# Retention and a gelu feed-forward in one kernel: the first four units in 128-token steps, with another load order

## The chip, the core and the metric

The kernel runs on one core of a Trainium2 chip. The metric is device time in microseconds (us). Four runs of the kernel before gave 297.36, 299.20, 298.86 and 299.65 us, median 299.03. The profile is that of the first of them.

A core has five engines that run beside each other: TensorE (PE in the profile, with its weight loads as PEld), VectorE (DVE), ScalarE (ACT), GpSimd (POOL) and SyncE (SP). They wait for each other through semaphores. TensorE writes its results to PSUM, eight banks of 128 partitions by 512 fp32 numbers, which DVE and ACT read. Here POOL issues the loads and SP the stores.

## What is computed

```
scale = 1/sqrt(64);  gamma[h] = 1 - 2^(-5-h)
scores = scale * q @ k^T                      # q, k, v: 8 batches, 8 heads, 576 tokens, 64 wide, fp32
ret    = (scores * gamma[h]^(i-j) for i >= j, else 0) @ v
x      = ret, heads side by side              # 4608 tokens x 512
h      = x @ w_in                             # 512 x 2048
out    = (h * sigmoid(1.702 h)) @ w_out       # 2048 x 512, fp32 out
```

The decay factorizes: a row is multiplied by gamma^i and v by gamma^-j. So attention can go in blocks, and all earlier blocks enter through one 64x64 state per head, the sum of k^T v.

## The kernel before, in words

The 4608 tokens are 36 units of 128. Four units make a chunk, and there are nine chunks. Units 0 to 3 are the first 512 tokens of batch 0, so each of them needs the state of the ones before. For a chunk, the up-projection makes 16 column blocks of 128 (`up`, L532, one block for all 512 tokens with four matmuls; `up_group`, L545, several blocks for some of the units), each followed by a gelu on ACT (L541, L555). Then `down` (L560) makes four output tiles of 128 tokens, and `down_out` copies and stores them. The attention of the units of the next chunk is placed between these matmuls by hand.

There is no planner. Every operation is written out in order by `op` (L41); each engine runs its own operations in that order, and the waits follow from the names that an operation reads and writes. TensorE waits for TensorE only where `after_ops` says so.

The change is in `lead_in` (L662), which loads and attends units 0 to 3 and makes chunk 0.

- Loads. SP loads k and q of unit 0 (`load_kq0`, L232). POOL issues, in one queue: v of unit 0; k, q, v of unit 1 (`load`, with `load_kq` L208 and `load_v` L222); `load_win(0)` (L251), which is 512 columns of w_in in two transfers, one for each 64 partitions; unit 2; `load_win(1)`; unit 3; `load_win(2)` and `(3)`; four transfers of w_out; then units 4 to 11. k and q are turned from fp32 into bf16 on the way, and so is w_in.
- Transposes. `transpose_pe` (L341) makes four 128x128 transposes of k, or of q, into a bank, and `transpose_copy` (L349) brings them to `kqT` on ACT or DVE.
- Scores. `scores` (L471): a unit is two halves of 64 tokens. Each half is scored with itself only: 16 matmuls of 64x64 over four tiles of the array, head halves to banks C and D. `scores_out` (L484) multiplies them by the causal mask on DVE into `pm`.
- States. `state_half` (L390) adds one half's k^T v to bank K (eight matmuls, L383), and ACT casts the bank into `kv` (L393). This is done after each half.
- `block1` (L589): `inter` (L446) multiplies each half's q by the state before that half (16 matmuls of 64x64; for the second half that is the state after the first); `values` (L492) adds scores times v in two phases, where the second phase waits for the last matmul of the first, so that two row halves of the array don't write the same part of a bank at once; between the phases stands the second half's state. `x_out` (L511) multiplies banks X and Y by gamma^i on DVE into `xT`, the input of the up-projection.
- `warm` (L652) is a filler: a matmul of zeros into a bank that nobody reads. L654 in the profile.

In `lead_in` the order on TensorE is: seven fillers, unit 0, unit 1, five fillers, up of blocks 0 to 3 for units 0 and 1, unit 2, blocks 4 to 7 for units 0 and 1, unit 3 with blocks 0 to 7 for unit 2 between its steps, blocks 8 to 11 for all four units, blocks 0 to 7 for unit 3, and blocks 12 to 15 whole. Then the down-projection of chunk 0 begins, with units 4 to 7 attended between its steps.

Of the kernel before, what the change touches and what calls it, by code (L numbers as in the profile page):

```python
# [6 lines left out]
AF = mybir.ActivationFunctionType  # L7
# [6 lines left out]
P = 128  # L14
# [110 lines left out]
def unit_info(u):  # L125
    pb, i = divmod(u, 9)
    if i < 4:
        return pb, 0, i
    if i < 8:
        return pb, 1, i - 4  # L130
    return pb, 2, 4
# [12 lines left out]
def head(pb, g, hh):  # L144
    return 4 * pb + 2 * g + hh
# [13 lines left out]
def bass_retnet_parallel__then__act_gelu_quick_kernel(  # L159
# [10 lines left out]
    with es:  # L170
        def sb(name, shape, dtype):
            return es.enter_context(nc.sbuf_tensor(name, shape, dtype))
# [9 lines left out]
        kqT = [sb(f"kqT{i}", [P, 2 * HP, P], BF16) for i in range(NQT)]  # L182
        vp = [sb(f"vp{i}", [P, H, DH], BF16) for i in range(NVP)]
        pm = [[sb(f"pm{i}_{hh}", [P, 512], BF16) for hh in range(2)] for i in range(2)]
        kv = sb("kv", [P, NKV, HP, DH], BF16)
        stm = sb("stm", [P, 8, HP, DH], FP32)
        xT = [sb(f"xT{i}", [P, 4, 512], BF16) for i in range(2)]
# [11 lines left out]
        def ps32(n):  # L199
            return bank[n].ap()  # L200
# [47 lines left out]
        def kq_pair(u, which, hp):  # L248
            return kqn[u % NLD][:, which, 2 * hp : 2 * hp + 2, :]

        def load_win(i):  # L251
            op("pool", lambda e: [e.dma_start(
                w_in_sb[64 * pb : 64 * pb + 64, :, 512 * i : 512 * i + 512],
                moe_w_in[256 * pb : 256 * pb + 256, 512 * i : 512 * i + 512].rearrange(
                    "(a d) n -> d a n", d=DH),
            ) for pb in range(2)], writes=[f"win{i}"], dma=f"d_win{i}", ndma=2)

        def load_wout(i):
            op("pool", lambda e: e.dma_start(
# [116 lines left out]
        def key(u, a):  # L376
            return (2 * u + a) % NKV

        def update(u, a, banks, col, first):
            sl = u % NLD  # L380
            for hp in range(HP):
                for hh in range(2):
                    op("pe", lambda e, hp=hp, hh=hh: e.matmul(  # L383
                        ps32(banks[a])[64 * hh : 64 * hh + 64, col + 64 * hp : col + 64 * hp + 64],
                        kqn[sl][64 * a : 64 * a + 64, 0, 2 * hp + hh, :],
                        vp[u % NVP][64 * a : 64 * a + 64, 2 * hp + hh, :],
                        start=first and hp == 0, stop=True, skip_group_check=True),
                       reads=[f"kq{sl}_0", f"vp{u % NVP}"], writes=[banks[a]])

        def state_half(u, a):  # L390
            pb, kind, c = unit_info(u)
            update(u, a, "KK", 0, c == 0 and a == 0)
            op("act", lambda e: e.activation(  # L393
                kv[:, key(u, a), :, :].rearrange("p a i -> p (a i)"), ps32("K")[:, 0:256], AF.Copy),
               reads=["K"], writes=[f"kv{key(u, a)}"])

        KB = "KE"

# [72 lines left out]
        def scores(u):  # L471
            qt = kqT[u % NQT]
            c0 = 256 * (u % 2)
            for hp in range(HP):
                for a in range(2):
                    for hh in range(2):
                        op("pe", lambda e, hp=hp, a=a, hh=hh: e.matmul(  # L477
                            ps32(SB[hh])[64 * a : 64 * a + 64, c0 + 64 * hp : c0 + 64 * hp + 64],
                            qt[64 * hh : 64 * hh + 64, hp, 64 * a : 64 * a + 64],
                            qt[64 * hh : 64 * hh + 64, HP + hp, 64 * a : 64 * a + 64],  # L480
                            skip_group_check=True),
                           reads=[f"T{u % NQT}_0", f"T{u % NQT}_1"], writes=[SB[hh]])
# [49 lines left out]
        def up(c, f, lo=0, hi=4, b=None):  # L532
            b = b or "AB"[f % 2]
            n0, n1 = P * lo, P * hi
            for a in range(4):
                op("pe", lambda e, a=a: e.matmul(  # L536
                    bank[b][:, n0:n1], w_in_sb[:, a, P * f : P * f + P], xT[c % 2][:, a, n0:n1],
                    start=(a == 0), stop=(a == 3)),
                   reads=[f"win{f // 4}"] + [f"x{c % 2}_{j}_{hh}" for j in range(lo, hi) for hh in range(2)],
                   writes=[b])  # L540
            op("act", lambda e: e.activation(  # L541
                gT[c % 2][:, f, n0:n1], bank[b][:, n0:n1], AF.Gelu_apprx_sigmoid),
               reads=[b], writes=[f"g{c % 2}_{f}_{j}" for j in range(lo, hi)])

        def up_group(c, f0, nf, lo, hi, b):  # L545
            n = P * (hi - lo)
            for i in range(nf):
                f = f0 + i
                for a in range(4):
                    op("pe", lambda e, a=a, f=f, i=i: e.matmul(  # L550
                        bank[b][:, n * i : n * i + n], w_in_sb[:, a, P * f : P * f + P],
                        xT[c % 2][:, a, P * lo : P * hi], start=(a == 0), stop=(a == 3), skip_group_check=True),
                       reads=[f"win{f // 4}"] + [f"x{c % 2}_{j}_{hh}" for j in range(lo, hi) for hh in range(2)],
                       writes=[b])
            op("act", lambda e: e.activation(  # L555
                gT[c % 2][:, f0 : f0 + nf, P * lo : P * hi],
                bank[b][:, 0 : n * nf].rearrange("p (f t) -> p f t", f=nf), AF.Gelu_apprx_sigmoid),
               reads=[b], writes=[f"g{c % 2}_{f}_{j}" for f in range(f0, f0 + nf) for j in range(lo, hi)])
# [22 lines left out]
            return op("sp", f, reads=[f"osb{i}_{n0}"], writes=[f"out{u}_{n0}"],  # L581
                      dma=f"d_o{i}_{n0}", ndma=len(unit_rows(u)))

        def score1(u):
            scores(u)
            scores_out(u, 1, 0)
            scores_out(u, 1, 1)

        def block1(u, xo=True):  # L589
            started.clear()  # L590
            inter(u, u % 2)
            o = values(u, u % 2, 0)
            if unit_info(u)[1] < 2:
                state_half(u, 1)
            values(u, u % 2, 1, [o])
            if xo:
                x_out(u, u % 2, 0)
                x_out(u, u % 2, 1)

        def ahead(j):  # L600
            if 2 * j < NU:
# [60 lines left out]
        def lead_in():  # L662
# [3 lines left out]
            iota_large()  # L666
            load_v(0)
            load(1)
            load_win(0)
            load(2)  # L670
            load_win(1)
            load(3)
            load_win(2)
            load_win(3)
            for i in range(4):
                load_wout(i)
            for u in range(4, NPE + 4):
# [11 lines left out]
            cast_kq0(1, "dve")  # L689
            transpose_pe(0, 0, "E")  # L690
            transpose_copy(0, 0, "E", "dve")
            warm(1)
            transpose_pe(0, 1, "B")
            transpose_copy(0, 1, "B", "dve")
            scale_v(0)
            warm(2)
            scores(0)
            scores_out(0, 1, 0)
            scores_out(0, 1, 1)
            gq_next(1)  # L700
            state_half(0, 0)
            transpose_pe(1, 0, "E")
            transpose_copy(1, 0, "E", "act")
            warm(2)
            transpose_pe(1, 1, "B")
            transpose_copy(1, 1, "B", "act")
            scale_v(1)
            block1(0)
            warm(1)
            scores(1)  # L710
            scores_out(1, 1, 0)
            scores_out(1, 1, 1)
            warm(4)
            state_half(1, 0)
            warm(2)
            block1(1)
            warm(5)
            up_group(0, 0, 2, 0, 2, "A")
            up_group(0, 2, 2, 0, 2, "B")
            transpose_pe(2, 0, "E")  # L720
            transpose_copy(2, 0, "E", "dve")
            warm(1, "C")
            transpose_pe(2, 1, "D")
            transpose_copy(2, 1, "D", "act")
            warm(3, "C")
            scores(2)
            scale_v(2)
            scores_out(2, 1, 0)
            scores_out(2, 1, 1)
            gq_next(2)  # L730
            warm(2)
            state_half(2, 0)
            warm(2)
            block1(2)
            gq_next(3)
            up_group(0, 4, 2, 0, 2, "A")
            up_group(0, 6, 2, 0, 2, "B")
            transpose_pe(3, 0, "E")
            transpose_copy(3, 0, "E", "dve")
            transpose_pe(3, 1, "D")  # L740
            transpose_copy(3, 1, "D", "act")
            scale_v(3)
            up_group(0, 0, 4, 2, 3, "A")
            scores(3)
            state_half(3, 0)
            scores_out(3, 1, 0)
            scores_out(3, 1, 1)
            up_group(0, 4, 4, 2, 3, "B")
            block1(3)
            up_group(0, 8, 2, 0, 2, "A")  # L750
            up_group(0, 10, 2, 0, 2, "B")
            up_group(0, 8, 2, 2, 4, "A")
            up_group(0, 10, 2, 2, 4, "B")
            up_group(0, 0, 4, 3, 4, "A")
            up_group(0, 4, 4, 3, 4, "B")
            gq_next(4)
            gq_next(5)
            for f in range(12, NF):
                up(0, f)
            def ahead45():  # L760
                ahead(2)
# [151 lines left out]
```

## Time and profile before

| what | value |
|---|---|
| median of the four runs | 299.03 us |
| the profiled execution | 297.36 us |
| its span, first to last instruction | 295.6 us |
| TensorE busy | 289.3 us, 98% |
| ACT, DVE, POOL busy | 133.1, 100.8, 108.1 us |
| first up-projection matmul of chunk 0 (L550) | 13.20 us |
| first down-projection matmul (L562) | 32.84 us |
| granted TensorE clock | 1.00 |

A page of the profile gives, for each engine, busy time and instruction count; then the span in 40 slices of 7.4 us with the busy share in tenths; then the chain that ended last, which goes from the last instruction back to whatever released it; then groups of instructions by line of code. A timeline row has a start and a length in us, the engine, the line, the operation, the tile written and the tiles read, the shapes, and in brackets how long the engine had been idle and who ended that. Matmuls are pipelined: a row's length includes the way through the array, so the pace is read from the starts.

### The profile page before, as it was taken

To read this page: it belongs to the slowest core of one execution; us is meant where nothing else is said; L and a number is where in the kernel's file an instruction comes from. 1 tells how busy PE (TensorE), PEld (TensorE's weight loads), DVE (VectorE), ACT (ScalarE), POOL (GpSimd) and SP (SyncE) were. 2 spreads that over 40 slices of the span, in tenths; PEclk is the share of its full clock that TensorE was granted. 3 is DMA by queue.
4 is the path that set the end of the run, shared out by engine and by line. 5 is a ranking of instruction groups with operands and counts; after the bars stand their busy time and mean duration, and the time that the engine had idled before them with its cause. 6 is when DMAs were issued, how large, how long until landed. Compare 5 with 4: busy or idle time off the path is not lost.

```text
span 295.6 us, 7921 instructions
## 1 busy us (share of the span) xinstructions
PE 289.3 (98%) x3584; PEld 141.7 (48%) x3584; DVE 100.8 (34%) x203; ACT 133.1 (45%) x233; POOL 108.1 (37%) x137
## 2 busy tenths in 40 slices
PE   7999999899999999999999999999999999999996
PEld 2578355775543454345434543454345434443344
DVE  7464046444571344034602470138004700410000
ACT  7456434563347324732464246423652375216511
POOL 9999498000960940390029301920090000000000
PEclk9999999999999999999999999999999999999999
DMA  9999999996999993699369926991993050110021
GB/s 163 180 208 206 206 234 249 235 148 144 159 226 188 137 219 112 120 178 166 99 127 140 192 90 144 158 200 50 171 100 97 27 137 0 38 73 35 0 73 71
DMA packets 117234, 40.63 MB, mean 137 GB/s; under 512 B 106064, under 2 KB 110416, under 8 KB 117200
## 3 DMA queue, kind: packets, MB, share of 16 engines
q0 software_dynamic: 80160, 22.81, 67.0%
q1 hardware_dynamic: 37040, 17.31, 22.0%
q8 instruction: 28, 0.46, 0.6%
q14 instruction: 6, 0.05, 0.1%
HBM read 36.70 MB, written 9.44 MB: 156 GB/s over the span
## 4 chain that ended last, share of the span: by engine, by line
PE 96%; DMA 2%; POOL 1%; issue 1%; DVE 0%; POOLq 0%
PE psA L562 22%; PE psB L562 21%; PE psA L536 17%; PE psB L536 17%; PE psB L550 4%; PE psA L550 4%; PE psX L461 2%; DMA kqn<-in_q_dram 2%; PE psA L654 1%; PE psC L477 1%; PE psY L499 1%; PE psX L499 1%; PE psK L406 1%; PE psD L477 1%; PE psE L406 1%
## 5 line engine op out<-in xcount | busy, mean ns | idle before, releaser
L214 POOL DMA_DIRECT2D kqn<-in_k_dram x39 | 35.3, 915 | 111.4 <-DMA kqT<-kqn 108.3
L562 PE MATMUL psA<-w_out_sb,gT 128*128 128x512 bf16 (+1 forms) x304 | 70.1, 374 | 0.0
L562 PE MATMUL psB<-w_out_sb,gT 128*128 128x512 bf16 (+1 forms) x288 | 64.6, 373 | 0.0
L536 PE MATMUL psA<-xT,w_in_sb 128*128 128x512 bf16 x232 | 59.5, 379 | 0.0
L536 PE MATMUL psB<-xT,w_in_sb 128*128 128x512 bf16 x232 | 59.5, 379 | 0.0
L524 DVE TENSOR_TENSOR xT<-psX,gq 128x512 bf16<-128x512 f32 x16 | 11.1, 692 | 120.5 <-PE psX L499 120.5
L430 ACT ACTIVATE kv<-stm 128x1024 bf16<-128x1024 f32 (+1 forms) x18 | 15.6, 866 | 68.4 <-DVE stm L421 68.4
L562 PEld LDWEIGHTS psB<-w_out_sb,gT 128*128 128x128 bf16 x288 | 27.8, 98 | 31.7 <-ACT gT L541 0.3
L562 PEld LDWEIGHTS psA<-w_out_sb,gT 128*128 128x128 bf16 x304 | 27.8, 98 | 31.5 <-ACT gT L541 2.5
L541 ACT ACTIVATE gT<-psB 128x512 bf16<-128x512 f32 x58 | 34.6, 597 | 15.3 <-PE psB L536 15.2
L541 ACT ACTIVATE gT<-psA 128x512 bf16<-128x512 f32 x58 | 34.6, 597 | 14.9 <-PE psA L536 14.9
L227 POOL DMA_DIRECT2D vn<-in_v_dram x40 | 37.4, 942 | 1.4 <-issue 1.3
L214 POOL DMA_DIRECT2D kqn<-in_q_dram x39 | 35.5, 921 | 0.0
L536 PEld LDWEIGHTS psA<-xT,w_in_sb 128*128 128x128 bf16 x232 | 18.6, 97 | 31.3 <-ACT gT L541 16.0
L536 PEld LDWEIGHTS psB<-xT,w_in_sb 128*128 128x128 bf16 x232 | 18.1, 97 | 32.0 <-ACT gT L541 15.7
L336 DVE TENSOR_TENSOR vp<-vn,vfac 128x512 bf16<-128x512 f32 x36 | 23.2, 685 | 16.4 <-DMA vn<-in_v_dram 16.4
L572 ACT ACTIVATE osb<-psB 128x512 f32<-128x512 f32 (+1 forms) x18 | 10.5, 585 | 21.5 <-PE psB L562 21.5
L572 ACT ACTIVATE osb<-psA 128x512 f32<-128x512 f32 x18 | 10.5, 584 | 15.3 <-PE psA L562 15.3
L486 DVE TENSOR_TENSOR pm<-psC,mask 128x512 bf16<-128x512 f32 (+1 forms) x20 | 12.6, 629 | 8.8 <-PE psD L477 8.7
L550 PE MATMUL psB<-xT,w_in_sb 128*128 128x256 bf16 (+1 forms) x128 | 14.8, 260 | 0.1
L550 PE MATMUL psA<-xT,w_in_sb 128*128 128x256 bf16 (+1 forms) x128 | 14.6, 259 | 0.0
L486 DVE TENSOR_TENSOR pm<-psD,mask 128x512 bf16<-128x512 f32 (+1 forms) x20 | 12.6, 628 | 0.0
(76 smaller groups left out, 257.2 us busy)
## 6 DMA issues: line engine op xcount, KB each, us to landing
vn<-in_v_dram POOLq DMA_DIRECT2D x32, 256.0 KB, 5.4
out_dram<-osb SPq DMA_DIRECT2D x31, 256.0 KB, 2.1
kqn<-in_k_dram POOLq DMA_DIRECT2D x31, 128.0 KB, 4.9
kqn<-in_q_dram POOLq DMA_DIRECT2D x31, 128.0 KB, 5.0
w_in_sb<-in_moe_w_in_dram POOLq DMA_DIRECT2D x8, 256.0 KB, 8.6
w_out_sb<-in_moe_w_out_dram POOLq DMA_DIRECT2D x4, 512.0 KB, 15.7
out_dram<-osb SPq DMA_DIRECT2D x10, 128.0 KB, 2.5
vn<-in_v_dram POOLq DMA_DIRECT2D x8, 128.0 KB, 5.1
```

Source lines behind the costliest of these rows:

```text
L214: e.dma_start(kqn[sl][p0 : p0 + n, which, :, :], src[b, :, s0 : s0 + n, :].rearrange("h p d -> p h d"),)
L227: e.dma_start(vn[sl][p0 : p0 + n, :, :], v[b, :, s0 : s0 + n, :].rearrange("h p d -> p h d"))
L336: op(eng, lambda e: e.tensor_tensor(vp[u % NVP].ap(), vn[sl].ap(), vfac[:, ty, :, None].to_broadcast([P, H, DH]), ALU.mult), reads=[f"vn{s ...
L406: op("pe", lambda e, hp=hp, a=a, hh=hh: e.matmul(ps32(KB[a])[64 * hh : 64 * hh + 64, c0 + 64 * hp : c0 + 64 * hp + 64], kqn[sl][64 * a : 6 ...
L430: op("act", lambda e: e.activation(kv[:, i0 % NKV : i0 % NKV + n, :, :], stm[:, i0 % 8 : i0 % 8 + n, :, :], AF.Copy), reads=[f"stm{(i0 + i ...
L486: op("dve", lambda e: e.tensor_tensor(pm[(u0 // 2) % 2][hh][:, c0:c1].rearrange("p (a i) -> p a i", i=64), ps32(SB[hh])[:, c0:c1].rearrang ...
L524: op("dve", lambda e: e.tensor_tensor(xT[ch % 2][:, slice(hh, 4, 2), P * jj : P * jj + 2 * P].rearrange("p g (u t) -> p u g t", u=2), ps32 ...
L536: op("pe", lambda e, a=a: e.matmul(bank[b][:, n0:n1], w_in_sb[:, a, P * f : P * f + P], xT[c % 2][:, a, n0:n1], start=(a == 0), stop=(a == ...
L541: op("act", lambda e: e.activation(gT[c % 2][:, f, n0:n1], bank[b][:, n0:n1], AF.Gelu_apprx_sigmoid), reads=[b], writes=[f"g{c % 2}_{f}_{j ...
L550: op("pe", lambda e, a=a, f=f, i=i: e.matmul(bank[b][:, n * i : n * i + n], w_in_sb[:, a, P * f : P * f + P], xT[c % 2][:, a, P * lo : P * ...
L562: op("pe", lambda e, f=f: e.matmul(bank[b][:, 0 : n1 - n0], gT[c % 2][:, f, P * r : P * r + P], w_out_sb[:, f, n0:n1], start=(f == 0), sto ...
L572: op("act", lambda e: e.activation(dst, src, AF.Copy), reads=[b], writes=[f"osb{i}_{n0}"])
```

## The change

Units 0 to 3 are attended as whole 128-token steps. The state goes from unit to unit only: `state1` adds a whole unit's k^T v at once (eight matmuls with all 128 tokens as rows) and `state1_cast` casts it once. `inter1` multiplies the q of all 128 tokens by the state after the unit before. What the second half takes from the first half of its own unit now comes from cross scores: `scores1` makes eight matmuls of 64x64 more into bank B, four before the usual sixteen and four behind them, where the second four wait for the last of the first four; `cross_out` copies them to a new tile `pmx` on ACT; `cross_values` multiplies them with v at the end of each phase of `values1`. The second phase waits for the last cross value of the first.

POOL's queue loads unit 2 right behind unit 1, then the columns of w_in for blocks 0 and 1, then unit 3, then blocks 2 and 3, 4 and 5, 6 and 7 in pairs, and 8 to 11 and 12 to 15 in fours as before. The wait of an up-projection is now for its own block's columns. The order on TensorE is written anew, with fillers at other places.

```diff
-        def load_win(i):
+        def load_win(f0, nf):
             op("pool", lambda e: [e.dma_start(
-                w_in_sb[64 * pb : 64 * pb + 64, :, 512 * i : 512 * i + 512],
+                w_in_sb[64 * pb : 64 * pb + 64, :, P * f0 : P * f0 + P * nf],
...
+        def state1(u):
...
+                        ps32("K")[64 * hh : 64 * hh + 64, 64 * hp : 64 * hp + 64],
+                        kqn[sl][:, 0, 2 * hp + hh, :], vp[u % NVP][:, 2 * hp + hh, :],
...
+        def scores1(u):
+            qt = kqT[u % NQT]
+            o = None
+            for hh in range(2):
+                if hh:
+                    scores(u)
+                wait = [o] if hh else ()
+                for hp in range(HP):
+                    o = op("pe", lambda e, hp=hp, hh=hh: e.matmul(
+                        ps32("B")[0:64, 256 * hh + 64 * hp : 256 * hh + 64 * hp + 64],
+                        qt[64 * hh : 64 * hh + 64, hp, 0:64],
+                        qt[64 * hh : 64 * hh + 64, HP + hp, 64:128], skip_group_check=True),
+                       reads=[f"T{u % NQT}_0", f"T{u % NQT}_1"], writes=["B"], after_ops=wait)
...
+        def cross_out(u):
+            dst = pmx[0:64, u % 2, :]
+            op("act", lambda e: e.activation(dst, ps32("B")[0:64, :], AF.Copy),
+               reads=["B"], writes=[f"pmx{u % 2}"])
...
+        def values1(u, phase, after_ops=()):
...
+            return cross_values(u, phase)
...
+        def block1(u):
             started.clear()
-            inter(u, u % 2)
-            o = values(u, u % 2, 0)
-            if unit_info(u)[1] < 2:
-                state_half(u, 1)
-            values(u, u % 2, 1, [o])
+            if u % 4:
+                inter1(u)
+            o = values1(u, 0)
+            values1(u, 1, [o])
+            x_out(u, u % 2, 0)
+            x_out(u, u % 2, 1)
...
             load(1)
-            load_win(0)
             load(2)
-            load_win(1)
+            load_win(0, 2)
             load(3)
-            load_win(2)
-            load_win(3)
+            load_win(2, 2)
+            load_win(4, 2)
+            load_win(6, 2)
+            load_win(8, 4)
+            load_win(12, 4)
```

The new order of `lead_in` from unit 0's scores to the down-projection (calls on TensorE, DVE and ACT in the order in which they are issued):

```
scores1(0); scores1_out(0, 0); scores1_out(0, 1); cross_out(0); warm(1, "A")
transpose_pe(1, 0, "E"); transpose_copy(1, 0, "E", "act"); state1(0); block1(0)
transpose_pe(1, 1, "A"); transpose_copy(1, 1, "A", "act"); state1_cast(0); scale_v(1); warm(2, "C")
scores1(1); scores1_out(1, 0); scores1_out(1, 1); cross_out(1); warm(1, "A")
transpose_pe(2, 0, "E"); transpose_copy(2, 0, "E", "act"); state1(1); gq_next(1); warm(1, "A"); block1(1)
transpose_pe(2, 1, "A"); transpose_copy(2, 1, "A", "act"); state1_cast(1); scale_v(2); warm(3, "C")
scores1(2); scores1_out(2, 0); scores1_out(2, 1); cross_out(2); gq_next(2); warm(3, "E"); block1(2)
gq_next(3); warm(2, "C"); up_group(0, 0, 2, 0, 2, "A")
transpose_pe(3, 0, "E"); transpose_copy(3, 0, "E", "dve"); transpose_pe(3, 1, "D"); transpose_copy(3, 1, "D", "dve")
scale_v(3); up_group(0, 0, 2, 2, 3, "B"); state1(2); state1_cast(2); warm(1, "C")
scores1(3); scores1_out(3, 0); scores1_out(3, 1); cross_out(3); warm(4, "E"); block1(3)
up_group(0, 2, 2, 0, 2, "A"); up_group(0, 2, 2, 2, 3, "B"); state1(3); state1_cast(3)
up_group(0, 0, 4, 3, 4, "E"); gq_next(4); gq_next(5); up(0, 4) to up(0, 15)
```

Here `up_group(c, f0, nf, lo, hi, bank)` makes blocks f0 to f0+nf-1 for units lo to hi-1. From the down-projection of chunk 0 on, nothing is changed.

## Prediction

> **What bounds the kernel now.** I read the page first: engine shares and slices, then the chain that ended last.
>
> ```profile
> PE 289.3 (98%) x3584; PEld 141.7 (48%) x3584; DVE 100.8 (34%) x203; ACT 133.1 (45%) x233; POOL 108.1 (37%) x137
> ...
> PE   7999999899999999999999999999999999999996
> ...
> DMA  9999999996999993699369926991993050110021
> ...
> PE 96%; DMA 2%; POOL 1%; issue 1%; DVE 0%; POOLq 0%
> ```
>
> TensorE is the bound and carries 96% of the chain; DMA carries 2%, all of it before 8.1 us (unit 1's q). So only what lengthens or shortens TensorE's own order counts. The change stops at the first down-projection: from there both orders are the same. The question is therefore when the first L562 row starts. In TensorE's timeline:
>
> ```profile
> 11.99 1.25 PE L654 MATMUL psA<-gT 128*128 128x512 bf16 x5
> 13.20 1.05 PE L550 MATMUL psA<-xT,w_in_sb 128*128 128x256 bf16 x8
> 14.08 1.04 PE L550 MATMUL psB<-xT,w_in_sb 128*128 128x256 bf16 x8
> 14.95 0.39 PE L344 MATMUL psE<-ident,kqn 128*128 128x128 bf16 x4
> ...
> 32.84 1.03 PE L562 MATMUL psA<-w_out_sb,gT 128*128 128x512 bf16 x4
> ```
>
> It starts at 32.84. Chunk 0's up-projection is 16 column blocks at 0.86 (starts 30.25, 31.11, 31.97): 13.8 us in either kernel. The other 19 us are attention for units 0 to 3, filler matmuls (L654), and waits; only these can change. The fillers here stand where unit 2's data is awaited. DVE's timeline shows that release:
>
> ```profile
> 16.12 0.69 DVE L336 TENSOR_TENSOR vp<-vn,vfac 128x512 bf16<-128x512 f32 x1 [0.32 <-DMA vn<-in_v_dram]
> ```
>
> The short rows I price with come from the end of unit 1's block:
>
> ```profile
> 11.35 0.21 PE L461 MATMUL psX<-kqT,kv 64*64 64x64 bf16 x1
> ...
> 11.53 0.19 PE L499 MATMUL psY<-pm,vp 64*64 64x64 bf16 x1
> 11.56 0.29 PE L383 MATMUL psK<-vp,kqn 64*64 64x64 bf16 x8
> 11.81 0.22 PE L499 MATMUL psY<-pm,vp 64*64 64x64 bf16 x2
> ...
> 11.87 0.20 PE L499 MATMUL psX<-pm,vp 64*64 64x64 bf16 x2
> 11.99 0.39 PE L654 MATMUL psA<-gT 128*128 128x512 bf16 x1
> ```
>
> Read starts, not lengths (matmuls overlap). Sixteen L461 take 0.14, eight L499 0.07, eight L383 0.11. A matmul that waits for an earlier TensorE matmul starts 0.28 after that one's start (11.53 to 11.81). Going back to full-array work costs 0.12 to 0.13 after the last start (11.87 to 11.99); going into 64-row work costs 0.09 (a filler at 11.04 occupies to 11.26, L461 starts 11.35). A filler occupies 0.22, four transposes 0.23. From TensorE's recorded end to ACT or DVE is 0.04, from DVE to TensorE 0.05, from ACT to TensorE 0.15 (a kqT copy ends 16.41, scores start 16.56). ACT's 128x512 copy is 0.60, its state cast 0.38; DVE's product of 128x256 is 0.42, and 0.34 after another.
>
> **Part by part.** Removed per unit: eight of sixteen state matmuls, one ACT cast of 0.38, and the wait of the second half's inter on that cast. Inter becomes eight matmuls of 128 columns: the same columns over the same four tiles, 0.14. All of this was beside other work except about 0.1 of issue.
>
> Added per unit: eight cross scores, an ACT copy of 64x512, eight cross values. None has a row.
> - Four cross scores go to one tile. Eight L383 on two tiles take 0.11, so four on one tile take 0.10 to 0.13 (ends: 0.03, the pace of the sixteen scores, and 0.8, four full lengths of 0.2). I take 0.13, the nearest row.
> - The second four wait for the first four (0.28 after the last start). The sixteen scores fill only part of that. From the first score at s: last cross score starts s+0.48, TensorE free for full-array work at s+0.61, against 0.25 for the scores alone (9.35 to 9.60): +0.36 a unit.
> - The cross copy lies between 0.38 (128x256) and 0.60 (128x512); I take 0.60, as its rows are 512 long. It ends at s+1.31, its values may start at s+1.46. DVE's products are done by s+1.25: ACT's copy becomes the later of the two.
> - Cross values: four on two tiles, 0.06 each time (ends 0.03 and 0.4). Behind the first four, in TensorE's order, stand phase 1's values, which wait 0.28; the half state that filled that wait is gone. TensorE is free at s+2.04 at the earliest.
>
> Now the walk, with the diff's fillers.
> - Unit 0 (s=6.35 as before): free 8.39. Transposes of unit 1's q stand behind this block now: 8.39, not 8.12 (q landed 8.1). ACT's copy ends 9.42, so unit 1's scores start 9.57, not 9.35.
> - Unit 1: two fillers, transposes, state, then the block at 11.26; free 12.05, where before had 11.99. No gain so far.
> - Transposes to 12.28, ACT copy to 13.08: unit 2's scores at 13.23, not 16.56. Here is the gain of the new load order, if the data is there. Three fillers follow; free 15.36, not 18.78.
> - Two fillers 0.43, an up pair 0.87, unit 3's transposes 0.46, an up pair of 128 columns 0.44, to 17.56. The gelu that reads bank B ends 18.15; the cross scores write B, so unit 3's scores start 18.30. Four fillers; free 20.65, not 24.02.
> - But by 24.02 the old order had done 8 column blocks for units 0 to 2, 8 x 0.65 = 5.2 of the 13.8. The new one has done 2, 1.3. Left: 12.5 of up and 0.34 for the last state excursion: 20.65 + 12.84 = 33.5.
>
> So the first down-projection starts at 33.5 instead of 32.84: **+0.7 us**. A cross-check on what comes after 12.0: both orders have 13 fillers there (2.8 us); new are 2 x 0.36 of scores, 2 x 0.15 of blocks and 0.2 of wait for the gelu, gone is a transpose group (0.23) and some 0.2 of other gaps: again +0.8 or less. The early data is taken up by fillers, because the up-projection that filled those places has moved behind it.
>
> **Transfers and queues.** Landing is issue plus the DMA view's latency in narrow windows. v of unit 1 lands 8.8 (4.19 + 4.6). A unit's three pieces took 2.4 (35.9 to 38.3, unit 4) to 3.3 (18.1 to 21.4, unit 3). POOL issues a piece each 0.88, 4.1 to 4.7 before it can land. So unit 2 lands by 11.2 to 12.1, its q by 10.3 to 11.3; needed 12.05. Column pairs have no row. By bytes a pair is half of 2.57 (w_out pieces land 28.2 to 35.9, three steps); small pieces cost up to 1.33 times that (k and q, 128 KB, land 0.8 to 0.85 apart against 0.64): 1.3 to 1.7 a pair. Running on: first pair 12.5 to 13.8 (needed 15.8), unit 3 14.9 to 17.1 (k needed 16.7, v 17.9), later pairs 16.2 to 18.8, 17.5 to 20.5, 18.7 to 22.2 (needed 20.7, 23.2, 24.9), the two quads by 24.8 and 27.3 (needed 26.6, 30.1), w_out's last by 37.5 (needed 38.7). All hidden; without that cover each late us is a us. POOL has four more issues of 0.65, 2.6 us: unit 4's first is issued at 20.8 rather than 18.15, still 16 before it lands. SP's orders are untouched, and its first transposes wait until 62.7.
>
> [...]
>
> **Sum.** Profiled execution 297.36, of which the span is 295.6. Span after 296.3, execution 298.1. The median shown is 299.03, 1.67 above that execution: 299.7.
>
> **Rivals.**
> - The new matmuls are nearer their low ends and their waits hide (cross scores 0.03, no wait, copies 0.38). For it: four-tile scores do run at 8 ns a start. Against: both waits are in the code, and 0.28 is the row in every block. Then fillers alone set the pace: units free at 11.6, 14.5 and 19.3, the first down-projection at 32.1, -0.7: 298.3. A measured gain over 0.5% needs more than that; 10%, with what I do not see.
> - The load order does not do what it says: unit 2's q stays late, because 2048 small packets for k and q set the pace and not their place. Decides from 12.05 on; each us beyond is one us. If q lands as before, at 15.0: +0.7 + 3.0, 302.7. For it: unit 1's q took 1.5 us after its k. Against: the queue served everything in issue order in this trace. 11%.
> - A column pair takes as long as a quad (cost per packet, not byte): 2.57 each, 5 us more in all. TensorE stands at the third pair (24.9) and at w_out's last piece, +2 to +3 in all: 302.4. Against: q of 128 KB lands in a third of a 512 KB piece's time. 5%.
> - My forecast, within 0.5%: 74%.
>
> **Numbers.** About 0.5% (1.5 us) is what a measurement of this kernel can tell from no change. Faster by more 0.10, within 0.74, slower by more 0.16. The range reaches from the low ends, 298.3 less 0.4 for the spread of medians (runs reach from 297.36 to 299.65), to +2: 297.9 to 301.2. That leaves out the late q, the slow pairs and a hidden gain.
>
> **What would show it.** In the new profile: unit 1's block ends about 12.0; unit 2's scores start about 13.2 after an ACT copy and not a DMA; the second cross scores start about 0.38 after the first; ACT's cross copy 0.6; the first down-projection starts at 33.5. DMA named as releaser of a TensorE row after 12 us would prove the transfer sum wrong; a down-projection before 32.5 would prove the walk's waits too long.

## The result, and the profile after

The changed kernel took 299.19 us (median of 53 runs, 298.24 to 305.85), the kernel before 297.92 (median of 79 runs, 296.65 to 300.62). The ratio is 1.0041, with a 95% interval of 1.0029 to 1.0053: about 1.2 us slower; two runs that are over 1.5% above the fastest (302.75 and 305.85) are left out of it. The profiled execution of the changed kernel took 299.44 us with a span of 297.6, against 297.36 and 295.6.

The page of the changed kernel: the busy line, two rows of the slices, the first line of the chain, and one group of the down-projection.

```profile
PE 290.0 (97%) x3532; PEld 138.9 (47%) x3532; DVE 101.2 (34%) x203; ACT 134.0 (45%) x234; POOL 110.5 (37%) x141
...
PE   7999999999999999999999999999979999999996
...
DMA  9999999998999995799349935992591150010021
...
PE 96%; issue 1%; DMA 1%; DVE 1%; ACT 0%
...
L560 PE MATMUL psA<-w_out_sb,gT 128*128 128x512 bf16 (+1 forms) x304 | 70.1, 374 | 1.5 <-issue 1.5
```

TensorE is still the bound, with 52 matmuls fewer. In the row of slices, the 8 in the eighth slice (51.7 to 59.1 us) has become a 9, and a new 7 stands in the thirtieth, 216 to 223 us, some 180 us behind the last line that was edited. The last line says what it is: one idle time of 1.5 us, with no releaser but "issue". The chain's DMA share fell from 2% to 1%.

In the lead-in, TensorE's timeline of the changed kernel, at the points that the walk named:

```profile
9.45 0.25 PE L590 MATMUL psB<-kqT 64*64 64x64 bf16 x2 [0.26 <-ACT kqT L355]
...
9.82 0.31 PE L590 MATMUL psB<-kqT 64*64 64x64 bf16 x4
10.06 0.39 PE L713 MATMUL psA<-gT 128*128 128x512 bf16 x1
...
11.17 0.24 PE L643 MATMUL psX<-kqT,kv 64*64 64x128 bf16 x1
...
11.90 0.28 PE L345 MATMUL psA<-ident,kqn 128*128 128x128 bf16 x2
...
33.22 0.59 PE L560 MATMUL psA<-w_out_sb,gT 128*128 128x512 bf16 x2
```

Read starts. Unit 1's scores take from 9.45 to 10.06, 0.61, with the second cross scores 0.37 behind the first. Its block takes from 11.17 to 11.90. The first down-projection starts at 33.22, 0.38 later than before (32.84).

That is only a fifth of the 2.0 us between the spans. After the first down-projection, where both kernels do the same work in the same order, the old one needs 295.6 - 32.84 = 262.8 us and the new one 297.6 - 33.22 = 264.4. The waits of TensorE that have no releaser, in the changed kernel (columns: total us, times, longest):

```profile
PE psA L560 <- issue: 1.5, 1, 1.5
...
PE psB L548 <- issue: 0.3, 1, 0.3
PE psC L345 <- issue: 0.3, 1, 0.3
...
PE psB L534 <- issue: 0.2, 1, 0.2
```

and in the kernel before:

```profile
PE psK L406 <- issue: 0.9, 1, 0.9
```

The longest of the new ones in the timeline of the changed kernel:

```profile
221.41 0.20 PE L497 MATMUL psX<-pm,vp 64*64 64x64 bf16 x2
223.12 0.39 PE L560 MATMUL psA<-w_out_sb,gT 128*128 128x512 bf16 x1 [1.50 <-issue]
```

From one start to the next are 1.70 us, in a place where the old kernel goes on without a gap:

```profile
220.90 0.20 PE L499 MATMUL psX<-pm,vp 64*64 64x64 bf16 x2
221.03 1.25 PE L562 MATMUL psA<-w_out_sb,gT 128*128 128x512 bf16 x5
```

I numbered TensorE's matmuls in both traces, with the first as 0. After the first 9 us, every place of this kind where a matmul starts over 0.2 us later than the pace stands at a number that leaves 88 to 90 when divided by 128: in the old kernel at 729 and 857 (51.5 and 59.2 us), in the new one at 602, 729, 1240 and 2904 (48.8, 56.7, 85.1 and 221.4 us). With its weight load a matmul is two instructions (3584 and 3584 on the page of before, 3532 and 3532 on that of the changed kernel), so the period is 256 instructions. What the start intervals there have above the pace of the matmul before them adds up to 1.31 us in the old kernel and 2.98 in the new one. Of the 1.70 at 221.41, though, the old kernel too spends 0.13 at this place (220.90 to 221.03), so these places make some 1.6 of difference. With the 0.38 of the lead-in that is the 2.0, but for a rest of 0.1.

The trace has a second witness. The queue called "instruction" that moves packets of 16,384 bytes moves 28 of them in the old kernel and 27 in the new one; 3584 and 3532 matmuls, with as many weight loads, are 28 and 27.6 blocks of 256. One such packet starts 2.2 to 2.45 us before TensorE goes on: at 220.79 for the gap that ends at 223.12, at 54.83 for 57.28, at 50.28 for 52.57 in the old kernel. I read it as the next block of TensorE's instructions arriving too late, and call these places, one in every 128 matmuls, bounds.

The large gap has one thing more to itself: the 128 matmuls ahead of matmul 2904 are all 64x64 and take 1.38 us, less than those 2.2. At every other such bound after the first 13 us, in both kernels, the 128 matmuls ahead take 3.5 us or more.

### The profile page after: what moved, and what is told of

Read it like the earlier page. It is cut to its first block, busy times and chain, and to the rows that moved or that the text cites. A ratio compares the mean times of both kernels' runs of the same rounds, so it can differ in the third digit from the quotient of the medians.

```text
span 297.6 us, 7823 instructions
## 1 busy us (share of the span) xinstructions
PE 290.0 (97%) x3532; PEld 138.9 (47%) x3532; DVE 101.2 (34%) x203; ACT 134.0 (45%) x234; POOL 110.5 (37%) x141
## 4 chain that ended last, share of the span: by engine, by line
PE 96%; issue 1%; DMA 1%; DVE 1%; ACT 0%
PE psA L560 22%; PE psB L560 20%; PE psA L534 18%; PE psB L534 18%; PE psA L548 3%; PE psB L548 3%; PE psX L459 2%; PE psC L475 1%; DMA osb<-in_k_dram 1%; PE psX L497 1%; PE psY L497 1%; PE psK L404 1%; PE psD L475 1%; PE psB L590 1%; DVE kqn L246 1%
## 5 line engine op out<-in xcount | busy, mean ns | idle before, releaser
L534 PE MATMUL psB<-xT,w_in_sb 128*128 128x512 bf16 x248 | 63.7, 379 | 0.2 <-issue 0.2
L534 PE MATMUL psA<-xT,w_in_sb 128*128 128x512 bf16 x248 | 63.7, 379 | 0.0
L539 ACT ACTIVATE gT<-psB 128x512 bf16<-128x512 f32 x62 | 37.0, 597 | 16.7 <-PE psB L534 16.6
L539 ACT ACTIVATE gT<-psA 128x512 bf16<-128x512 f32 x62 | 37.0, 597 | 16.1 <-PE psA L534 16.1
L534 PEld LDWEIGHTS psA<-xT,w_in_sb 128*128 128x128 bf16 x248 | 19.8, 97 | 33.7 <-ACT gT L539 17.0
L534 PEld LDWEIGHTS psB<-xT,w_in_sb 128*128 128x128 bf16 x248 | 19.5, 97 | 34.4 <-ACT gT L539 17.0
L484 DVE TENSOR_TENSOR pm<-psC,mask 128x512 bf16<-128x512 f32 x16 | 10.9, 682 | 8.2 <-PE psE L404 8.2
L419 DVE TENSOR_TENSOR stm<-psE,stm 128x256 f32<-128x256 f32 x28 | 11.9, 424 | 1.2
L484 DVE TENSOR_TENSOR pm<-psD,mask 128x512 bf16<-128x512 f32 x16 | 10.9, 681 | 0.0
```

What stands on the lines that cost most here:

```text
L419: op("dve", lambda e: e.tensor_tensor(dst, src, prev, ALU.add), reads=[KB[a], f"stm{(i - 1) % 8}"], writes=[f"stm{i % 8}"])
L484: op("dve", lambda e: e.tensor_tensor(pm[(u0 // 2) % 2][hh][:, c0:c1].rearrange("p (a i) -> p a i", i=64), ps32(SB[hh])[:, c0:c1].rearrang ...
L534: op("pe", lambda e, a=a: e.matmul(bank[b][:, n0:n1], w_in_sb[:, a, P * f : P * f + P], xT[c % 2][:, a, n0:n1], start=(a == 0), stop=(a == ...
L539: op("act", lambda e: e.activation(gT[c % 2][:, f, n0:n1], bank[b][:, n0:n1], AF.Gelu_apprx_sigmoid), reads=[b], writes=[f"g{c % 2}_{f}_{j ...
```

## The theories, and the experiments

**Theory: the count.** The edits shift the rest of the program against blocks of 256 TensorE instructions. Ahead of the first down-projection are 456 matmuls in the old kernel and 404 in the new one. With another count, other parts of the program stand at the block bounds, and a bound behind many short matmuls stalls. If so, a count of 456 must take the gap near 221 us out of the new kernel and 404 + 128 = 532 must bring it into the old one, whatever the order is.

**Rival: the order.** The lead-in itself does it: other transfers, other times at which buffers come free; or the gap is an accident of one execution. Then the count is without effect.

**For the lead-in**: the walk says that fillers stand where work could, and that the load order pays only with the new order. That is tried by moving work, and by giving each kernel the loads of the other.

All kernels below compute the whole result. Ratios are to the kernel before, run on the same chip.

### a_shift: the new kernel with 456 matmuls

Eighteen of the later fillers are cut into four or two narrower matmuls, with the same columns in all: 52 more.

```diff
+        parts = iter([1] * 7 + [4] * 17 + [2])
...
+                m = next(parts, 1)
+                w = 512 // m
+                for j in range(m):
+                    op("pe", lambda e, j=j, w=w: e.matmul(
+                        bank[b][:, w * j : w * j + w], gT[1][:, 0, 0:P], gT[1][:, 0, w * j : w * j + w],
```

> The changed kernel with 18 of its 21 later fillers cut into four (17) or two (1) matmuls of fewer columns: 52 matmuls more over the same columns, so 3584 in all and 456 before the first down-projection, as in the kernel before; every later matmul then has the number it had before. In the two profiles the long idle times of TensorE after 33 us that no semaphore explains lie at matmuls 729 and 857 (before) and 602, 729, 1240 and 2904 (changed), all at 88 to 90 modulo 128, that is every 256 TensorE instructions counting weight loads; together 1.31 us before and 2.98 us changed. Theory fetch: these are instruction blocks arriving late, and their place depends on the count of instructions alone; of the 2.0 us between the two profiles 0.4 is the lead-in and 1.6 this. It expects the first down-projection at 33.2 to 33.4, the idle 1.5 before matmul 2904 gone, idle times again at 729 and 857, and a ratio to the kernel before of 1.001 to 1.0025. Rival lead-in: the lost time comes from the new order and its transfers, the count does nothing: ratio 1.004 as the changed kernel, the idle time at 221 us stays.

Median 298.78 us, ratio 1.0022 (0.9993 to 1.0051). The first down-projection starts at 33.28, as in the changed kernel (33.22), the span is 295.9 instead of 297.6, and there is no gap near 221. TensorE's longest wait without a releaser stands now where the kernel before has it, at L404 (L406 there):

```profile
PE psK L404 <- issue: 0.7, 1, 0.7
```

It starts at matmul 729 and 51.94 us; in the old kernel it was matmul 729 at 51.50. The count alone moved the gaps from one kernel's pattern to the other's.

### b_shift: the old kernel with 532 matmuls

The same cut in the old kernel, `parts = iter([1] * 6 + [2] + [4] * 25)`: 76 more.

> The kernel before with its 25 later fillers cut into four matmuls each and one of the first seven into two: 76 matmuls more over the same columns. 76 more is the same as 52 fewer modulo 128, so the block bounds fall on the same matmuls after the first down-projection as in the changed kernel, while order, loads and lead-in are those of before. Theory fetch expects idle times of 0.3 to 0.5 at about 49, 57 and 85 us and of up to 1.7 near 221 us, and a ratio to the kernel before of 1.003 to 1.006. Rival lead-in expects 1.000 to 1.001, no more than the 0.1 us that the cut fillers cost.

Median 300.86 us, ratio 1.0106 (1.0085 to 1.0127), more than expected. The gap near 221 is there (1.02 us, at matmul 3032 = 2904 + 128). But TensorE also waits inside the lead-in now. Its waits, of which the third is the gap near 221:

```profile
PE psB L550 <- issue: 1.0, 1, 1.0
...
PE psB L550 <- ACT gT L555: 0.9, 1, 0.9
PE psA L562 <- issue: 0.8, 1, 0.8
```

The first stands at 14.96 to 16.23 us between two equal up-projection matmuls. The second, at 28.75 to 29.89, is put down to ACT; since it stands at the next such bound, I take that for the label of a wait that was over, but that is argued. The first down-projection starts at 36.00, 3.2 later; of that, 0.8 was there before either wait, since the first up-projection matmul waits for w_in and starts at 13.97 instead of 13.20. So more than one thing has changed, and the size says nothing on the count alone. The next pair of kernels puts its extra matmuls elsewhere.

### a_late and b_late: the extra matmuls behind the lead-in

In a_late the fillers are left as they are, and blocks 11 to 15 of chunk 0's up-projection are cut in four (the last in two) by columns: 52 more.

```diff
+        cuts = iter([1] * 7 + [4] * 4 + [2])
...
+            m = next(cuts, 1) if c == 0 else 1
+            w = (n1 - n0) // m
+            for j0 in range(n0, n1, w):
```

> The changed kernel with its lead-in and fillers untouched; five of the last whole column blocks of chunk 0's up-projection (blocks 11 to 15) have their matmuls cut into four (the last one into two) of fewer columns, which adds 52 matmuls after 28 us over the same columns, so that later matmuls have the numbers of the kernel before. Theory fetch expects the first down-projection at 33.2 to 33.4, no idle time near 221 us, idle times at matmuls 729 and 857, a span of 295.8 to 296.1 and a ratio to the kernel before of 1.001 to 1.002. Rival lead-in: the changed kernel's 297.6 and 1.004.

Median 298.53 us, ratio 1.0014 (0.9989 to 1.0038); first down-projection at 33.34, span 295.9. The gap near 221 is gone, and one at matmul 729 (52.01 us, 1.14) has come, as in a_shift; at 857, which was expected too, there is none. Up to block 11, so up to 28 us, the order is that of the changed kernel, instruction for instruction: this tells against the rival.

b_late cuts the old kernel's up-projection in the same way, only after 24 us, for 76 more:

```diff
+        cuts = iter([4] * 4)
...
+                if c == 0 and f0 >= 8 and gcuts[0] < 7:
+                    m, gcuts[0] = 2, gcuts[0] + 1
```

> The kernel before with its lead-in, loads and fillers untouched up to 24 us; 76 matmuls are added after that by cutting matmuls of chunk 0's up-projection (seven pairs of 256 columns into halves, blocks 12 to 15 into four) over the same columns. 76 more is 52 fewer modulo 128. The first run of this kind also moved block bounds inside the lead-in and lost 2.4 us there; this one does not. Theory fetch expects the first down-projection at 32.8 to 33.1 (or 1.1 later if the bound at matmul 473, which falls among the cut ones, is idle again), idle times near 49, 57, 85 and 221 us as in the changed kernel, and a ratio to the kernel before of 1.003 to 1.006 (1.009 with that bound). Rival lead-in: 1.000 to 1.001.

Median 299.97 us, ratio 1.0062 (1.0037 to 1.0087). The gap is there, in the old kernel:

```profile
222.16 0.20 PE L499 MATMUL psX<-pm,vp 64*64 64x64 bf16 x2
223.57 0.60 PE L574 MATMUL psA<-w_out_sb,gT 128*128 128x512 bf16 x2 [1.21 <-issue]
```

The ratio is larger than the gaps make it. In the profiled execution the first down-projection is 1.5 us late (34.38), since unit 1's v landed at 10.93 instead of 8.78, ahead of all that was edited. Whether that was so in all its runs can't be seen from one profile. So b_late shows that the gap follows the count, and not its price.

### a_lean: work in place of fillers

The order of the changed kernel with three edits: the single fillers ahead of unit 1's state and of its block go; the two fillers behind unit 2's block go; and the up pair of blocks 2 and 3 for units 0 and 1 takes the place of the four fillers ahead of unit 3's block. Four other fillers are cut so that the count stays 404.

```diff
-            warm(1, "A")
...
-            warm(1, "A")
...
-            warm(2, "C")
...
-            warm(4, "E")
-            block1(3)
             up_group(0, 2, 2, 0, 2, "A")
+            block1(3)
```

> The changed kernel without the two single fillers of unit 1 and the two after unit 2's block, and with the up pair of blocks 2 and 3 for units 0 and 1 in the place of the four fillers ahead of unit 3's block; four other fillers are cut so that the number of matmuls before the first down-projection stays 404. The walk says that these fillers, not the data, hold TensorE: it expects the down-projection 0.3 + 0.43 + 0.87 = 1.6 us earlier, at 31.6 (before 32.84, changed 33.22), with the idle times after it where the changed kernel has them: ratio to the kernel before 0.998 to 1.000. Rival: the fillers stand where data is awaited (w_in pairs or unit 3), so their removal only turns them into waits named after a DMA: down-projection at 32.8 to 33.2, ratio 1.003 to 1.004.

Median 297.62 us, ratio 0.9999 (0.9977 to 1.0021). TensorE's timeline at unit 3 shows work where fillers stood:

```profile
17.89 0.31 PE L590 MATMUL psB<-kqT 64*64 64x64 bf16 x4
18.14 1.05 PE L548 MATMUL psA<-xT,w_in_sb 128*128 128x256 bf16 x8
19.11 0.24 PE L643 MATMUL psX<-kqT,kv 64*64 64x128 bf16 x1
...
31.98 0.59 PE L560 MATMUL psA<-w_out_sb,gT 128*128 128x512 bf16 x2
```

The first down-projection starts at 31.98, 1.24 ahead of the changed kernel and 0.86 ahead of the old one, where 31.6 was expected. What the two fillers of unit 1 brought went to unit 1's q: it landed at 8.84 in this execution, 0.58 later than in the changed kernel's profile, and TensorE waited 0.5 us for it. Unit 1's scores start 0.52 later (9.97 instead of 9.45), but its block ends as early (11.88 and 11.90). And the block bounds still take about 2.0 us (from 220.05 to the next start 1.32).

### a_lean_shift: the same with 456

All its fillers are cut in four: `parts = iter([4] * 20)`.

> The same leaner order with all fillers cut into four, 456 matmuls before the first down-projection and 3584 in all, as in the kernel before. Theory fetch with the walk expects both gains: down-projection at 31.7, idle times at matmuls 729 and 857 alone, ratio to the kernel before 0.995 to 0.998. Rival lead-in expects the ratio of the leaner order without the cut.

Median 297.09 us, ratio 0.9972 (0.9956 to 0.9987); first down-projection 31.96, span 294.8, with one gap of 1.14 at matmul 729. This version is faster than both kernels: the early data, with the order that uses it, is worth some 0.8 us if work replaces fillers and the bounds fall as in the old kernel.

### a_oldload and b_newload: each kernel with the other's loads

a_oldload has the new order of work with the old load order and sizes; b_newload has the old order of work with the new loads and the wait on one's own columns. The edit in a_oldload, of which b_newload is the mirror:

```diff
             load(1)
+            load_win(0, 4)
             load(2)
-            load_win(0, 2)
+            load_win(4, 4)
             load(3)
-            load_win(2, 2)
-            load_win(4, 2)
-            load_win(6, 2)
```

> The changed kernel's computation in its own order, with POOL's loads in the order and the sizes of the kernel before (w_in in four pieces of 512 columns, the first two ahead of units 2 and 3). The walk expects unit 2's transposes of k to wait for the load until 14.0 and of q until 15.0, v scaled at 16.8, its scores at 16.8 instead of 12.98, and from there the rest 3.8 to 4.0 later: first down-projection at 37.0 to 37.3, ratio to the kernel before 1.013 to 1.016. Rival: the load order matters little, because the fillers and the up pairs take up what is late: first down-projection below 34.

Median 305.6 us, ratio 1.0237 (1.0202 to 1.0272), more than expected: the first down-projection is 2 us later than the wait for the data makes it. In TensorE's timeline:

```profile
14.48 0.61 PE L345 MATMUL psE<-ident,kqn 128*128 128x128 bf16 x4 [3.86 <-DMA kqn<-in_k_dram]
...
17.37 1.49 PE L713 MATMUL psC<-gT 128*128 128x512 bf16 x3
```

and by stretches of the span (the stretch and its length, busy time of PE, PEld, DVE, ACT and POOL with instruction counts, granted clock, DMA share and GB/s):

```profile
9.00:14.00 5.00, 1.36 (x27) 0.62 (x25) 2.30 (x6) 1.44 (x3) 5.00 (x8) 0.86 1.54 177
14.00:17.00 3.00, 2.46 (x46) 1.57 (x47) 0.01 (x1) 0.60 (x1) 3.00 (x6) 0.50 1.37 203
17.00:18.90 1.90, 1.90 (x14) 0.79 (x13) 1.34 (x3) 0.87 (x2) 1.90 (x3) 0.50 1.95 213
18.90:33.00 14.10, 13.98 (x214) 8.83 (x214) 6.79 (x16) 6.50 (x13) 13.44 (x17) 0.98 1.25 209
```

The granted clock is 1.00 until 12.5 us and 0.50 from 12.7, within the idle time. It stays at 0.50 behind it, from 14.48 until about 19.4 us, 4.9 us long (the 0.98 of the last stretch is its first half microsecond), and a filler takes 0.43 us instead of 0.22. At half speed 4.9 us do the work of 2.45. With the late data this puts the first down-projection at 39.19 instead of 37.0 to 37.3. That the 3.9 us of idle time brought the 4.9 us at half rate is my reading of this one profile; in b_newload, below, TensorE was idle for 2.39 us and the granted clock from 12 to 33 us is 1.00.

> The kernel before in its own order of computation, with POOL's loads in the order and sizes of the changed kernel. The walk expects the up pair of blocks 0 and 1 to wait for w_in until 14.3 and that of blocks 2 and 3 until 17.8, in front of unit 2, whose data has long landed: unit 2's scores at 20.3 instead of 16.56 and the first down-projection 3.6 to 3.8 later, at 36.4 to 36.7, ratio 1.012 to 1.014. Rival: unit 2's earlier data makes up for it: first down-projection at 33 to 34.

Median 300.68 us, ratio 1.0084 (1.0053 to 1.0115), less than expected. The profiled executions differ by the 3.6 us that were expected (300.94 and 297.36), the medians by 2.7. The second up pair of the old order wants columns that the new loads bring later:

```profile
14.69 1.04 PE L550 MATMUL psA<-xT,w_in_sb 128*128 128x256 bf16 x8
...
18.11 1.05 PE L550 MATMUL psB<-xT,w_in_sb 128*128 128x256 bf16 x8 [2.39 <-DMA w_in_sb<-in_moe_w_in_dram]
```

The first down-projection starts at 36.84. In this execution unit 0's q landed at 5.87 instead of 4.6 us and its scores started 1.4 later, but the wait for w_in took that up: from this second pair to the down-projection it is 18.73 us (18.11 to 36.84), against 18.76 in the old kernel (14.08 to 32.84). Behind it the count is 456, and the rest takes 262.3 us. So neither half of the change stands alone: the order without the loads costs 2.4%, the loads without the order 0.8%, and both together 0.4%.

### All ten profiles by the count

| kernel | matmuls ahead of the first down-projection | its start, us | from there to the end, us | gap near 221 us |
|---|---|---|---|---|
| before | 456 | 32.84 | 262.8 | none |
| a_shift | 456 | 33.28 | 262.6 | none |
| a_late | 456 | 33.34 | 262.6 | none |
| a_lean_shift | 456 | 31.96 | 262.8 | none |
| b_newload | 456 | 36.84 | 262.3 | none |
| after | 404 | 33.22 | 264.4 | 1.70 |
| a_lean | 404 | 31.98 | 263.9 | 1.32 |
| a_oldload | 404 | 39.19 | 264.4 | 2.14 |
| b_shift | 532 | 36.00 | 263.1 | 1.02 |
| b_late | 532 | 34.38 | 263.7 | 1.40 |

The gaps are from one start to the next; without one that is 0.13. The fourth column is the span less the third. With 456 it lies between 262.3 and 262.8 whatever the order, the loads and the start are; with 404 or 532, which leave the same remainder by 128, between 263.1 and 264.4. That the gaps follow the count is shown. In measured time the evidence is weaker: a_shift (1.0022) and a_late (1.0014) are below the changed kernel's 1.0041, but their intervals overlap its own. Two more kernels in the leaner order, with 420 and 436 matmuls, gave no result, so no other remainder was measured. The smaller gaps don't follow the count alone: with 404, matmul 1240 starts late in two kernels and not in a_lean; with 456, 857 does in two of five.

The remark on the 128 matmuls ahead holds in all ten. The five kernels with the gap near 221 have a bound behind 128 matmuls that take 1.38 us; at all other bounds after the first 13 us it is 3.5 us or more. With 456, a bound falls inside that stretch of 64x64 matmuls.

## Why the prediction was right or wrong

The forecast, slightly slower and within 0.5%, held: 299.7 forecast, 299.19 measured, in a range of 297.9 to 301.2. Its +0.7 was measured as +1.2, but the two are not made of the same terms, and that they lie so close is in part luck: the lead-in cost less than forecast, and something cost time that the forecast didn't have. The absolute figure has luck too. It starts from 299.03, the median of four runs of the kernel before; 79 runs have 297.92, and from there +0.7 would have given 298.6.

- **The lead-in** was forecast at +0.7 (down-projection at 33.5) and is +0.38 (33.22). Two terms were mis-sized. The wait from ACT to TensorE was taken as 0.15; here it is 0.05: unit 2's kqT copy ends at 12.93 and the scores start at 12.98. It stands ahead of the scores of units 1 and 2, and the walk's lead grew with it: unit 1's scores were forecast at 9.57 and start at 9.45, unit 2's at 13.23 and 12.98. Unit 3's, forecast at 18.30, keep that lead and start at 18.01, 0.15 behind the end of the gelu that reads bank B (17.86). And the block was to cost 0.15 more; it takes 0.73 where the old one took 0.64 (11.35 to 11.99), +0.09.
- **The scores** were right: 0.61 a unit, of which +0.36 is new, with the wait on TensorE's own matmul where it was put (0.25 from start to start, 9.57 to 9.82, where 0.28 was taken).
- **The ACT copy** was right at 0.60, and it is the later of the two, as said. ACT's and DVE's timelines for unit 2:

```profile
12.33 0.60 ACT L355 ACTIVATE kqT<-psA 128x512 bf16<-128x512 bf16 x1 [1.03 <-PE psA L345]
...
13.69 0.59 ACT L606 ACTIVATE pmx<-psB 64x512 bf16<-64x512 f32 x1 [0.49 <-PE psB L590]
```

```profile
13.82 0.41 DVE L598 TENSOR_TENSOR pm<-psD,mask 128x256 bf16<-128x256 f32 x1
```

  The first line is also the answer on the releaser: unit 2's scores wait for an ACT copy, not for a DMA.
- **The transfers** were right but for one. Unit 2's q landed at 10.65 (forecast 10.3 to 11.3), its v at 11.87 (11.2 to 12.1), unit 3's v at 16.85 (up to 17.1), the later column pairs at 17.84, 19.2 and 20.56 (16.2 to 18.8, 17.5 to 20.5, 18.7 to 22.2), the last columns at 25.95 (by 27.3). The first pair landed at 14.28, 0.5 behind its range (12.5 to 13.8), but its matmuls start at 15.51, so nothing waited. The last two pairs are 1.36 apart. No DMA releases a TensorE row after 12 us. Four more pieces moved the last columns only from 25.69 to 25.95: the pieces of w_in land 4.2 us or more behind their issue, but a pair lands 1.36 behind the one before, so they overlap. The rivals of the late q and of the slow pair fall with that.
- **The rival that the waits hide**, first down-projection at 32.1, did not occur: the new waits are in the rows, and units 1 to 3 are free at 11.90, 15.07 and 20.29, not at 11.6, 14.5 and 19.3.
- **The step that failed** is a sentence of the first part: "from there both orders are the same". The order is; its time is not. The late starts at the bounds (matmul numbers that leave 88 to 90 when divided by 128) cost some 1.6 us more in the profiled execution. Of the 1.27 between the medians (299.19 - 297.92), 0.38 would be the lead-in and some 0.9 the bounds, if the profiled lead-in is typical. The trace of before could have raised the question: it had a wait of 0.9 put down to "issue" at matmul 729, and the change takes out 52 matmuls.

After the first 9 us TensorE starts over 0.2 us late at 2 of 28 bounds in the kernel before and at 4 of 27 in the changed one; the longest in the ten profiles is 2.14 us from start to start (a_oldload), and these few decide.

**Open.** Why the smaller stalls come at some bounds and not at others. For the large one the 1.38 us of the block ahead set it apart, which fits a block that comes too late but was not tested by itself. The others don't go by that time: they stand behind 128 matmuls that take 4.3 to 8.1 us, and bounds behind 3.5 us pass without one. That the missing thing is the next block of instructions rests on the period, on the number of packets and on the one that starts 2.2 to 2.45 us before; no run took the packet away. How large the gaps are outside the profiled executions wasn't measured either.

## What to carry to other kernels

When data comes earlier, ask what work can take the place of the wait: here fillers took it, and the change lost; with an up-projection pair in their place and a better count it gained (ratio 0.9972). In this long unrolled program a change in the number of early instructions moved idle times some 190 us behind the edit. So look for idle times of the bound engine without a releaser, number the instructions, and see whether they share a period. Test such a cause by splitting an instruction where it is cheap and far from the edit.

## What the runs showed of the hardware that was not expected

- Delays of TensorE put down to "issue", up to 2.14 us from start to start, stand in the ten profiles after the first 9 us only where the matmul number leaves 88 to 94 when divided by 128. Whether the largest occurs follows the count of matmuls ahead; it stands behind a block of 128 matmuls that take 1.38 us.
- In 3.9 us of idle time of TensorE in a_oldload the granted clock fell from 1.00 to 0.50, and TensorE then ran 4.9 us at it.
- The first landings differ from one profiled execution to the next: unit 1's q from 7.7 to 9.0 us, its v from 8.6 to 10.9. A few tenths at the start of one profile are no basis for a verdict.
